# Another order of the pieces of a fused attention and gated-convolution kernel, with one more pair's exponentials done row by row on ScalarE

## The chip, the cores and the metric

The kernel runs on one core of a Trainium2 chip. The metric is the device time of one execution in microseconds (us), the median of several runs. A profiled execution has a span (from the first to the last instruction of the core) and a time of its own, which is about 2 us longer.

## The reference, cut to what matters

```python
# 8 batches, 8 heads, 576 tokens, 64 values a head; chunks of 64 tokens
scores = scale * np.matmul(q_c, k_c.transpose(0, 1, 2, 4, 3))      # 64 x 64 a chunk and head
scores = scores - np.max(scores, axis=-1, keepdims=True)
attn = np.exp(scores)
attn = attn / (np.sum(attn, axis=-1, keepdims=True) + 1e-09)
out = np.matmul(attn, v_c)                                         # all heads side by side: x
for k in range(5):                                                 # causal convolution along the tokens
    gate_pre += conv_w[k] * xp[:, k:k + S, :]
gate = 1.0 / (1.0 + np.exp(-gate_pre))
result = (gate * (x @ w_val)) @ w_out                              # 512 x 512 weights, fp32
```

## The kernel before

The 4608 tokens are cut into nine groups of 512 (g, 0 to 8) and the 512 columns into two halves of 256 (p, 0 and 1). A group and a half make a **pair**. The work is written as some thousand **pieces**, and a table, `ORDER`, lists them in the order in which they are recorded; on each engine the instructions stand in that order, and semaphores do the rest. A second table, `SLOTS`, gives each new tile its place in SBUF (z), in PSUM (b, four double banks) and among the two buffers of exponentials (e). What a piece does, by its letters:

- `lq`, `lk`, `lv`, `lw`, `lc` load q, k, v, a quarter of a weight matrix (v for w_val, o for w_out), the convolution's weights. All loads and stores are issued on SyncE, in the table's order.
- `w1` to `w9`, `wa`, `wb`, `wc`, `Q` split a weight into a high part (`v_hi`, `o_hi`) and a low part (`v_lo`, `o_lo`).
- `S g p b` makes the scores of half a pair on TensorE (16 small matmuls of 64 by 64, which the hardware runs as 32). `mx` takes the maxima on VectorE. Then one of two ways: `sb`, `ex`, `sm` subtract on VectorE, take one wide exponential on ScalarE, and sum and invert on VectorE; or `ng`, `ea`, `rc` negate the maxima on VectorE, take the exponential on ScalarE in 16 instructions, one for each block of 64 columns, each of which also leaves its sum, and add 1e-9 and invert on VectorE. `nm` multiplies by the inverse (GpSimd, or VectorE as `nmD`).
- `T` transposes on TensorE, `ec` copies out on ScalarE, `A` multiplies by v on TensorE (64 small hardware matmuls for a pair).
- `xr` (ScalarE) and `xd` (VectorE) split x into high and low, `xc` keeps it for the convolution. `k0`, `k`, `kx`, `kk` are the five taps of the convolution, `hc` and `hb` hand the last tokens of a group on, `sg` is the sigmoid.
- `V g m c` multiplies by w_val: three matmuls of 512 columns (high by high, low by high, high by low), or one of them where a fifth number stands. `vc` copies the result out, `gs` multiplies by the gate, `gr` and `gd` split that into high and low, `P g t c` multiplies by w_out (three matmuls), `oc`, `o1` copy out, `st`, `s1` store.
- `W n m` is n matmuls of 512 columns and m of 64 on zeros. They stand at the start, before there is data.

A D at the end of a name puts a piece on VectorE that is else on ScalarE or GpSimd. In the trace almost all instructions have the line of the helper that records them (L139); they are told apart by their tiles: `b<-z,v_hi` is V, `b<-o_hi,z` is P, the matmuls `b<-z,z`, `b<-z,ys`, `b<-ys,z`, `b<-ys` of 64 by 64 are S and A, `b<-ident,z` is T, `e_row<-b,mx` is `ea`, `rs<-e_row` is `sm`.

## Time and profile before

| | |
|---|---|
| median of three runs | 280.42 us (280.19 to 280.89) |
| the profiled execution, its own time | 280.77 us |
| its span | 278.7 us |
| granted TensorE clock, mean | 0.999 |
| busy: TensorE matmul / VectorE / ScalarE / GpSimd | 97% / 86% / 71% / 21% |
| chain that ended last | TensorE 90% of the span |

An engine's busy time is what its instructions cover; matmuls overlap in the records, so TensorE at 97% says only that it was hardly ever without one in flight. The rows on which the prediction rests stand further on, word for word.

### The profile page before, as it was taken

The page shows a single profiled execution, that of the slowest core. Times are in us where ns is not written, and L with a number is a line of the kernel's source. Part 1 is how long each engine was busy: PE and PEld are TensorE (multiplying, and loading weights), DVE is VectorE, ACT ScalarE, POOL GpSimd, SP SyncE. Part 2 cuts the span into 40 slices and gives each one's busy share as a digit, 9 for nine tenths or more (in the row PEclk, how much of TensorE's full clock was granted, in tenths as well). Part 3 has the DMA queues.
Part 4 walks back from the last instruction along what each step waited for, and adds up shares of the span by engine and source line. Part 5 has one row for each costly group of instructions (what it writes and reads, how often), then busy time and mean ns, then how long its engine had stood idle before and what let it go on. Part 6 is the DMA issues. An engine that isn't in the chain of part 4 may idle for free.

```text
span 278.7 us, 7853 instructions
## 1 busy us (share of the span) xinstructions
PE 269.3 (97%) x3370; PEld 216.7 (78%) x3370; DVE 240.6 (86%) x305; ACT 198.2 (71%) x366; POOL 59.5 (21%) x58
## 2 busy tenths in 40 slices
PE   8589999999999999999999999999999999999995
PEld 3357788887887878798888888888888888888884
DVE  3999999999999989988998998999999998996020
ACT  5989999999988998895968588828634544614402
POOL 1056242059293003062325001100000000300000
PEclk9999999999999999999999999999999999999999
DMA  6999999763821449440081000000000000050656
GB/s 226 394 407 406 407 409 405 301 231 121 308 104 67 162 157 368 158 154 6 2 308 70 2 5 2 0 0 2 0 0 0 4 0 0 23 205 0 245 206 226
DMA packets 14754, 42.46 MB, mean 152 GB/s; under 512 B 1536, under 2 KB 1792, under 8 KB 14720
## 3 DMA queue, kind: packets, MB, share of 16 engines
q1 hardware_dynamic: 14720, 41.97, 40.3%
q8 instruction: 26, 0.43, 0.6%
q14 instruction: 8, 0.07, 0.1%
HBM read 32.53 MB, written 9.44 MB: 151 GB/s over the span
## 4 chain that ended last, share of the span: by engine, by line
PE 90%; DVE 4%; DMA 2%; ACT 1%; issue 1%; SPq 0%; DVEq 0%; ACTq 0%
PE b L139 90%; DMA z<-in_moe_w_val 2%; ACT e_row L139 1%; DVE z L139 1%; DVE rs L139 1%; DVE mx L139 1%; DVE e_row L139 1%; SPq L139 0%; ACT z L139 0%; DVE cw_h L139 0%; DVE cw_t L139 0%; DVEq L139 0%; DVE v_hi L139 0%; ACTq L139 0%
## 5 line engine op out<-in xcount | busy, mean ns | idle before, releaser
L139 PE MATMUL b<-z,v_hi 128*128 128x512 f32 x288 | 97.3, 403 | 0.8 <-issue 0.6
L139 PE MATMUL b<-o_hi,z 128*128 128x512 f32 (+1 forms) x296 | 94.5, 390 | 0.0
L139 DVE SCALAR_TENSOR_TENSOR ys<-ys,cw 128x511 f32<-128x511 f32 (+7 forms) x104 | 84.5, 863 | 0.1
L139 ACT COPY z<-b 128x1024 f32<-128x1024 f32 (+2 forms) x53 | 50.2, 969 | 37.6 <-PE b L139 34.9
L139 PEld LDWEIGHTS b<-o_hi,z 128*128 128x128 f32 x296 | 55.1, 188 | 12.7
L139 PEld LDWEIGHTS b<-z,v_hi 128*128 128x128 f32 x288 | 53.8, 188 | 14.0 <-issue 1.4
L139 PE MATMUL b<-o_lo,z 128*128 128x512 f32 (+1 forms) x148 | 57.4, 388 | 0.0
L139 PE MATMUL b<-z,v_lo 128*128 128x512 f32 x144 | 55.9, 394 | 0.0
L139 POOL TENSOR_TENSOR z<-e_row,rs 128x1024 f32<-128x1024 f32 (+1 forms) x15 | 27.0, 1804 | 46.4 <-DVE rs L139 20.0
L139 PEld LDWEIGHTS b<-o_lo,z 128*128 128x128 f32 x148 | 27.8, 188 | 5.9
L139 PEld LDWEIGHTS b<-z,v_lo 128*128 128x128 f32 x144 | 27.1, 188 | 5.4
L139 POOL TENSOR_TENSOR z<-ys,z 128x1024 fp32r<-128x1024 f32 x4 | 10.1, 2525 | 96.9 <-ACT z L139 96.9
L139 ACT ACTIVATE ys<-ys 128x1024 f32<-128x1024 f32 x16 | 16.8, 1060 | 11.0 <-DVE ys L139 10.8
L139 ACT ACTIVATE e_row<-b,mx 128x64 f32<-128x64 f32 x80 | 23.7, 354 | 0.4 <-DVE mx L139 0.4
L139 DVE TENSOR_TENSOR z<-b,z 128x1024 fp32r<-128x1024 f32 (+1 forms) x19 | 22.0, 1160 | 2.0 <-ACT z L139 1.4
L139 ACT CAST z<-ys 128x1024 fp32r<-128x1024 f32 x16 | 16.5, 1048 | 9.0 <-DVE ys L139 9.0
L139 DVE TENSOR_REDUCE mx<-b 128x16 f32<-128x1024 f32 (+1 forms) x19 | 21.5, 1139 | 1.2 <-PE b L139 1.0
L139 PEld LDWEIGHTS b<-z,z 64*64 64x64 f32 x960 | 15.6, 134 | 6.2 <-issue 2.2
L139 ACT CAST z<-b 128x1024 fp32r<-128x1024 f32 (+1 forms) x19 | 18.7, 991 | 2.1 <-PE b L139 2.1
L139 ACT ACTIVATION_READ_ACCUMULATOR e_row<-b,mx 128x1 f32 x80 | 19.7, 247 | 0.0
L139 PE MATMUL b<-z,z 64*64 64x64 f32 x960 | 17.4, 221 | 2.3 <-DMA z<-in_q 2.2
L139 ACT ACTIVATE ys<-ys,cw 128x512 f32<-128x512 f32 (+1 forms) x25 | 19.2, 812 | 0.0
(73 smaller groups left out, 309.9 us busy)
## 6 DMA issues: line engine op xcount, KB each, us to landing
out<-z SPq DMA_DIRECT2D x16, 512.0 KB, 3.7
z<-in_q SPq DMA_DIRECT2D x10, 512.0 KB, 7.1
z<-in_v SPq DMA_DIRECT2D x9, 512.0 KB, 4.8
ys<-in_v SPq DMA_DIRECT2D x9, 512.0 KB, 10.1
ys<-in_k SPq DMA_DIRECT2D x9, 512.0 KB, 6.3
z<-in_k SPq DMA_DIRECT2D x7, 512.0 KB, 9.9
ys<-in_q SPq DMA_DIRECT2D x6, 512.0 KB, 10.2
z<-in_moe_w_val SPq DMA_DIRECT2D x4, 512.0 KB, 5.4
```

The costliest lines, as they stand in the source:

```text
L139: return tc.keep_in_program_order(fn(*args, **kwargs))
```

## The change

Both tables are replaced. The pieces are the same but for these: pair 8 1 takes its exponentials row by row (`ng`, `ea`, `rc`, with `nm` on GpSimd) where it took `sb`, `ex`, `sm` and `nmD`; some pieces change their engine (`k0` of pairs 4 0, 4 1, 5 0, 5 1 go to VectorE, `kx 6 1` and `k0 8 2` leave it; `xc 6 1`, `oc 7 1`, `gd 3 1`, `waD o 1`, `wbD o 3` go to VectorE, `xc 3 0`, `oc 4 1`, `oc 6 0`, `o1 8 3`, `gd 8 0`, `wa o 3` leave it); and the zeros' matmuls are `W 12 22` where they were `W 9 22` and, later, `W 3`. The code around the tables is the same.

```diff
-ORDER = """zw,lw v 1,zr 1,zr 0,lc,zi,zs 0,zs 1,lw v 3,lw v 2,w1 v 1,w5 c 0,w1 c 0,w2 v 1,w3 v 1,w5 v 1,w4 v 1,w2 c 0,w3 c 0,w5 v 3,
-w7 v 1,w1 v 3,w6 v 1,w8D v 1,w2 v 3,w4 c 0,w3 v 3,W 9 22,Q v 1,lk 0 1 0,lq 0 1 0,w1 v 2,w4 v 3,w2 v 2,w3 v 2,w5 v 2,w6D v 3,
-S 0 1 0,lk 0 0 0,lk 0 1 1,lq 0 1 1,lq 0 0 0,lk 0 0 1,lq 0 0 1,w4 v 2,wc v 1,mx 0 1 0,w6 v 2,w7 c 0,ng 0 1 0,w7 v 2,ea 0 1 0,
...
+ORDER = """zw,lw v 1,zr 1,zi,zs 0,zs 1,lc,lw v 3,lw v 2,zr 0,lq 0 1 0,lk 0 1 0,lq 0 1 1,lk 0 1 1,w1 v 1,lk 0 0 0,w1 c 0,w3 c 0,w2 v 1,
+w3 v 1,w5 v 1,w4 v 1,w2 c 0,w7 v 1,w1 v 3,w8D v 1,w2 v 3,w3 v 3,w6 v 1,w4 c 0,w1 v 2,w2 v 2,w3 v 2,w4 v 3,w5 v 3,W 12 22,
+S 0 1 0,w7 c 0,w4 v 2,w5 c 0,w5 v 2,mx 0 1 0,w6 v 2,S 0 1 1,lq 0 0 0,lk 0 0 1,lq 0 0 1,lw v 0,ng 0 1 0,w7 v 2,ea 0 1 0,
...
-    e="0 1 0 0 0 0 1 1 0 0 0 1 0 1 1 0 1 0",
+    e="0 1 0 0 0 0 1 1 0 0 0 1 0 1 1 1 0 0",
```

Three places show what moves. The first is TensorE from the first full scores of group 1 on, some 19 to 27 us into the trace of before. Before, it reads (the rows are `S 1 0 0` and `S 1 0 1`, `A 0 1 0`, `T 0 1 1`, `V 0 2 2 0`, `V 0 3 2 1`, `A 0 1 1`, `T 0 0`, three V, `S 1 1 0`, `A 0 0`, `S 1 1 1`):

```order
L139 MATMUL b_315<-z_269,z_271 64x64 x32
L139 MATMUL b_356<-z_353,z_273 64x64 x16
L139 MATMUL b_307<-ident,z_295 128x128 x4
L139 MATMUL b_393<-z_390,v_hi 128x512
L139 MATMUL b_393<-z_390,v_lo 128x512
L139 MATMUL b_399<-z_353,z_273 64x64 x16
L139 MATMUL b_419<-ident,z_388 128x128 x8
L139 MATMUL b_393<-z_390,v_hi 128x512 x2
L139 MATMUL b_393<-z_390,v_lo 128x512
L139 MATMUL b_439<-z_373,z_375 64x64 x16
L139 MATMUL b_459<-z_434,z_377 64x64 x32
L139 MATMUL b_439<-z_373,z_375 64x64 x16
```

And now (the rows are `S 1 0 0` and `S 1 0 1`, `T 0 1 1`, `A 0 1 0`, `A 0 1 1`, `T 0 0`, seven V, `A 0 0`, `S 1 1 0` and `S 1 1 1`):

```order
L138 MATMUL b_311<-z_228,z_226 64x64 x32
L138 MATMUL b_305<-ident,z_292 128x128 x4
L138 MATMUL b_357<-z_350,z_288 64x64 x16
L138 MATMUL b_382<-z_350,z_288 64x64 x16
L138 MATMUL b_402<-ident,z_377 128x128 x8
L138 MATMUL b_414<-z_380,v_hi 128x512
L138 MATMUL b_416<-z_380,v_hi 128x512
L138 MATMUL b_414<-z_380,v_lo 128x512
L138 MATMUL b_416<-z_380,v_hi 128x512
L138 MATMUL b_414<-z_380,v_lo 128x512
L138 MATMUL b_414<-z_380,v_hi 128x512 x2
L138 MATMUL b_443<-z_436,z_427 64x64 x32
```

Seven V now stand ahead of `A 0 0`, where two then three stood on either side of `A 0 1 1` and `T 0 0`, and the two halves of `S 1 1` have moved behind `A 0 0`. Between `S 1 1 1` and `T 1 0`, the next transposes, 14 single V stood before and 13 stand now.

The second place is TensorE at 80 to 85 us, where the scores of pair 5 1 and `A 3 1` stand side by side. Before, `V 3 0 0` followed them:

```order
L139 MATMUL b_1328<-o_hi,z_1211 128x512
L139 MATMUL b_1372<-ys 64x64 x32
L139 MATMUL b_1407<-z_1367,ys 64x64 x32
L139 MATMUL b_1446<-z_1349,v_hi 128x512
L139 MATMUL b_1446<-z_1349,v_lo 128x512
L139 MATMUL b_1446<-z_1370,v_hi 128x512
```

Now `P 0 3 3` does:

```order
L138 MATMUL b_1321<-o_hi,z_1229 128x512
L138 MATMUL b_1366<-ys 64x64 x32
L138 MATMUL b_1403<-z_1362,z_719 64x64 x32
L138 MATMUL b_1321<-o_hi,z_1113 128x512
L138 MATMUL b_1321<-o_lo,z_1113 128x512
L138 MATMUL b_1321<-o_hi,z_1243 128x512
```

The small matmuls have kept their place and number; three other wide ones follow.

The third place is ScalarE at 150 to 160 us, around the exponentials of pair 8 1, with copies out of PSUM on both sides. Before (`ex 8 1` is the second row):

```order
L139 ACTIVATE ys<-ys,cw 128x512
L139 ACTIVATE e_row_65<-e_row_65 128x16x64
L139 COPY z_2351<-b_2338 128x1024
L139 COPY z_2384<-b_2224 128x1024
L139 COPY z_2389<-b_2176 128x1024
```

Now (`ea 8 1` is the third row):

```order
L138 ACTIVATE ys<-ys,cw 128x512
L138 COPY z_2334<-b_2321 128x1024
L138 ACTIVATE e_row_65,rs_2340<-b_2204,mx_2295 128x64 x16
L138 CAST z_2448<-b_2381 128x2x2x256
L138 COPY z_2467<-b_2310 128x1024
```

Sixteen instructions stand where one stood, between the copy `ec 8 0` and the copies `xr 7 0` and `vc 4 1`.

## Rows read from the trace of the kernel before

**Rows 1.** The page's busy times, its slices of 7 us each, and its list of DMA queues (packets, MB, share of 16 engines).

```profile
PE 269.3 (97%) x3370; PEld 216.7 (78%) x3370; DVE 240.6 (86%) x305; ACT 198.2 (71%) x366; POOL 59.5 (21%) x58
...
DMA  6999999763821449440081000000000000050656
...
q8 instruction: 26, 0.43, 0.6%
```

**Rows 2.** The windows of 10 us: stretch, its length, then each engine's busy time with the number of its instructions, the granted clock, the share of the DMA engines and GB/s.

```profile
0.00:10.00 10.00, 7.09 (x67) 3.27 (x67) 5.56 (x16) 6.43 (x13) 0.79 (x8) 1.00 0.80 274
10.00:20.00 10.00, 7.57 (x183) 4.91 (x176) 9.39 (x20) 8.55 (x39) 3.35 (x3) 1.00 1.04 406
20.00:30.00 10.00, 9.65 (x223) 7.72 (x224) 9.33 (x16) 9.79 (x16) 6.39 (x4) 1.00 1.03 407
...
80.00:90.00 10.00, 9.38 (x166) 7.58 (x165) 9.27 (x13) 8.15 (x11) 5.96 (x5) 1.00 0.08 27
...
150.00:160.00 10.00, 10.00 (x172) 8.44 (x170) 9.93 (x12) 6.36 (x8) 0.83 (x1) 1.00 0.01 2
```

**Rows 3.** TensorE from 80 to 86 us in the timeline (start, duration, engine, line, operation, tiles, shapes, count, and the idle time before it).

```profile
81.37 1.16 PE L139 MATMUL b<-ys 64*64 64x64 f32 x64
...
83.39 0.50 PE L139 MATMUL b<-z,v_hi 128*128 128x512 f32 x1
...
83.72 0.39 PE L139 MATMUL b<-z,v_lo 128*128 128x512 f32 x1
...
84.74 0.50 PE L139 MATMUL b<-z,v_hi 128*128 128x512 f32 x1 [0.62 <-issue]
```

**Rows 4.** DMA queue 8 in short stretches: of 28.8 to 28.9 us, of 82.0 to 82.1 us, and of 28.8 to 30 us.

```profile
q8 instruction: 1, 0.02, 64.5%
...
q8 instruction: 1, 0.02, 79.9%
...
q8 instruction: 1, 0.02, 5.4%
```

**Rows 5.** Matmuls in four of the stretches asked for (length, busy time and count of the matmuls, clock, DMA share, GB/s).

```profile
19.33:25.05 5.72, 5.26 (x143) 1.00 1.03 407
25.05:31.23 6.18, 6.12 (x142) 1.00 1.03 407
...
81.38:84.74 3.36, 2.73 (x132) 1.00 0.02 5
84.74:104.86 20.12, 20.12 (x124) 1.00 0.42 141
```

**Rows 6.** The first 31 us in the timeline.

```profile
1.19 4.67 PE L139 MATMUL b<-warm 128*128 128x512 bf16 x31 [1.19 <-DVE warm L139]
...
9.41 0.69 PE L139 MATMUL b<-z,z 64*64 64x64 f32 x32 [0.73 <-DMA z<-in_q]
...
11.36 0.31 ACT L139 ACTIVATE e_row<-b,mx 128x64 f32<-128x64 f32 x1 [0.25 <-DVE mx L139]
...
11.40 1.37 PE L139 MATMUL b<-z,z 64*64 64x64 f32 x64 [0.54 <-DMA z<-in_q]
...
11.66 0.30 ACT L139 ACTIVATE e_row<-b,mx 128x64 f32<-128x64 f32 x1
...
13.84 1.27 POOL L139 TENSOR_TENSOR z<-z,z 128x512 fp32r<-128x512 f32 x1 [12.45 <-ACT e_row L139]
13.87 1.27 DVE L139 TENSOR_SCALAR rs<-rs 128x8 f32<-128x8 f32 x1 [0.17 <-ACT e_row L139]
...
15.29 1.18 DVE L139 TENSOR_REDUCE mx<-b 128x16 f32<-128x1024 f32 x1
...
18.31 0.16 DVE L139 TENSOR_SCALAR rs<-rs 128x8 f32<-128x8 f32 x1
...
18.92 1.24 DVE L139 TENSOR_REDUCE rs<-e_row 128x16 f32<-128x1040 f32 x1 [0.21 <-ACT e_row L139]
...
20.68 1.90 POOL L139 TENSOR_TENSOR z<-e_row,rs 128x1024 f32<-128x1024 f32 x1 [0.77 <-DVE rs L139]
...
24.14 1.02 ACT L139 COPY z<-b 128x1024 f32<-128x1024 f32 x1 [0.21 <-issue]
```

**Rows 7.** The same stretch, TensorE alone, as the timeline merges it.

```profile
18.73 1.96 PE L139 MATMUL b<-z,z 64*64 64x64 f32 x96 [0.23 <-DMA z<-in_q]
...
23.00 1.06 PE L139 MATMUL b<-ident,z 128*128 128x128 f32 x8 [0.25 <-DVE e_row L139]
23.82 0.71 PE L139 MATMUL b<-z,v_hi 128*128 128x512 f32 x2
...
24.69 2.15 PE L139 MATMUL b<-z,z 64*64 64x64 f32 x128
26.77 0.50 PE L139 MATMUL b<-z,v_hi 128*128 128x512 f32 x1
...
30.14 1.03 PE L139 MATMUL b<-ident,z 128*128 128x128 f32 x8
31.23 0.74 PE L139 MATMUL b<-z,v_hi 128*128 128x512 f32 x2
```

**Rows 8.** Groups of instructions (line, engine, operation, tiles, shapes, count, busy us, mean ns of one, idle time before them): `ex`, and `k0` with `kx` on ScalarE.

```profile
L139 ACT ACTIVATE e_row<-e_row 128x1024 f32<-128x1024 f32 x13 | 13.9, 1071 | 2.9 <-DVE e_row L139 2.9
...
L139 ACT ACTIVATE ys<-ys,cw 128x512 f32<-128x512 f32 (+1 forms) x25 | 19.2, 812 | 0.0
```

## The prediction, made before the changed kernel ran

> **What bounds the kernel now.** First the page's busy times and the windows: TensorE's matmuls cover 97% of the span, and from 30 us on all of every window but that of 80 to 90 us [rows 1, 2]. The table changes no matmul: 3370 stand before and after. So the time can move only where TensorE stands still: before 31 us, at 84 us, and after its last matmul, where copy and store keep their order. The other engines count where they make it wait.

> The other place is the start. The stretch from 25.05 to 31.23 is also one block [rows 5]; its packet starts between 28.8 and 28.9 and lasts 1.03 us [rows 4], and the next matmul after the transposes that begin at 30.14 starts at 31.23, 1.35 after the packet's end [rows 7]. Eight transposes take 0.82 when nothing holds them (23.00 to 23.82 [rows 7]), so TensorE lost some 0.3 there. With the DMA engines full (share 1.03) a block takes 3.8 + 1.03 + 1.35 = **6.18 us**; the block before it took 5.72 [rows 5].

> [...]

> **The change, the start.** I follow the new order with the durations of before.
> - `S 0 1 0` waits for its q at 9.41 [rows 6]; the same bytes stand ahead of it now, so 9.4 again.
> - `S 0 1 1` started at 11.40, after its q [rows 6]. Its two transfers of 256 KB now go ahead of a third one, 0.65 us at 406 GB/s [rows 2]: 10.7.
> - One cast less stands before the first maxima on VectorE, so `ea 0 1 0` starts at about 11.0, where it was 11.36 [rows 6].
> - The maxima of pair 0 0 started at 15.29 because a tiny instruction took 1.27 us at 13.87, beside GpSimd's 1.27 at 13.84; the same instruction later takes 0.16 [rows 6]. Now it falls ahead of GpSimd's: the maxima start when `S 0 0 1` is there, 14.2, and the sums that started at 18.92 [rows 6] start at 18.0.
> - `S 1 0 0` waited for its q until 18.73 [rows 7], the fifteenth transfer; its k is now the fifteenth, so 18.7 again.
> - `nm 0 0` on GpSimd started at 20.68 [rows 6]; now at 19.5, and `T 0 0` at 21.75 (it was 23.00 [rows 7]).
> - ScalarE copies that out (24.14 for 1.02 [rows 6]) from 23.7, behind three other copies, and `A 0 0` starts at 24.8.

> So VectorE gains 0.9 us and `A 0 0` some 0.4. But TensorE counts in blocks: the block that ended 0.36 into `S 1 1 0` (24.69 + 0.36 = 25.05 [rows 7]) now ends 0.3 into `A 0 0`, at **25.1**, because two more V stand ahead of it. The next holds the rest of `A 0 0`, `S 1 1` and 13 single V, and ends at the sixth transpose of `T 1 0`: 108 of the 128 small matmuls that took 2.08 (24.69 to 26.77), 13 of the 14 V that took 3.37 (26.77 to 30.14), and 0.6 of transposes [rows 7]: 1.76 + 3.13 + 0.6 = 5.5 us. The fetch takes 6.18 if it waits in the full queues as before, 5.72 if as in the block before. I take 6.18, the nearest row, since the queues are as full in both: 25.1 + 6.18 = 31.28 against 31.23, **+0.05**. The gain goes into a longer wait for the fetch, 0.7 for 0.3. With no such wait it is 30.6, -0.65; with one 0.3 longer, +0.35.

> **The change, at 84 us.** The block starts in `S 5 1 0` as before and ends in the third matmul of `P 0 3 3` instead of that of `V 3 0 0`. The same two scores and `A` lie in between, so the work is 2.6 us again and the wait 0.8: **0**. Bounds: -0.8 if the fetch is early, +0.2 for a later packet.

> **The rest.** 16 instructions of `ea 8 1` at 0.30 from start to start (11.36 to 11.66 [rows 6]) put 4.8 us on ScalarE and take a 1.07 away [rows 8]; `sb`, `sm` and `nmD` take three of some 1.2, as the one at 18.92 [rows 6], from VectorE, and `nm` puts one of 1.9, as the one at 20.68 [rows 6], on GpSimd. Four `k0` leave ScalarE, 0.8 each [rows 8]; on VectorE they cost from nothing to as much. The other changes of engine nearly cancel. So ScalarE gets some 2 to 4 us more and VectorE up to 4 less. What covers it: ScalarE is busy 6.36 of the 10 us at 150 to 160 while TensorE stands nowhere [rows 2]. Behind `ea 8 1` wait `xr 7 0` and `vc 4 1`, for which `T 7 1` needs the bank; by the order V pieces of 0.7 fill the time and about 1 us is left. If that cover is gone, each us late is a us: bounds 0 and +1. Value **0**. The wide matmuls go from small ones and back about as often (22 runs of small ones in each table): **-0.1**.

> **The sum.** Against the profiled execution: 280.77 + 0.05 + 0 + 0 - 0.1 = 280.7. Its time is 0.35 over the median of the runs, 280.42. So the median should be **280.4**.

> **The rivals.**
> 1. *The fetches no longer hold TensorE*: packets that start early let the block of `T 1 0` end at its work, 30.6, and that of `P 0 3 3` at 2.6. -0.65 - 0.8 - 0.1: **278.9**. For it: a block took 5.72 once, and packets start 0.65 after a block's end in quiet queues. Against it: the loads keep the queues full (share 1.03 to 50 us [rows 1, 2]), and at 84 us nothing was left to be quieter (share 0.02 [rows 5]).
> 2. *The clock falls in the new gap; slower.* `W 12 22` ends at about 6.4: nine matmuls of 0.43 to 5.0, three of half that, 22 short ones. From there to 9.41 TensorE has nothing; before, it had `Q v 1` in that stretch and `W 3` behind the first scores, and the granted clock stayed up [rows 2]. [...] It decides if the clock is down at 18.7. For it: 3 us without work is more than any stretch of before. Against it: the rows show no fall at all, though TensorE did little from 5.86 (1.19 + 4.67) to 9.41 [rows 6]. [...]
> 3. *Another block is squeezed; slower.* From `S 7 0 0` to `P 2 3 3` the new order has 26 + 32 + 64 small matmuls and six wide ones: 122 x 0.0163 (2.08/128) + 6 x 0.24 = 3.4 us, just over the 3.36 that a fetch needs. If stores or loads still fill the queues at 128 us, the fetch needs up to 6.2, and TensorE stands 2.8: **283.2**. For it: the queues were 4 to 9 tenths full from 105 to 125 us [rows 1], and transfers may now come later. Against it: they were all but empty from 125 to 139.

> **How the numbers follow.** Not told from no change by a measurement of this kernel: 0.3%, 0.84 us. Forecast, 280.4 with 279.6 to 281.2: 0.45. Rival 1: 0.27. Rival 2: 0.12. Rival 3: 0.08. Left: 0.03 faster, 0.05 slower by some copy that comes late. Faster 0.30, same 0.45, slower 0.25. The range goes 0.4 beyond the middle of rivals 1 and 2, 278.5 to 282.8: a quarter of rival 1 lies below it, a third of rival 2 and all of rival 3 above, two in ten in all.

> **What would show it.** Right: `S 0 1 1` at 10.7, `T 0 0` at 21.7, `A 0 0` at 24.8, and the matmul behind `T 1 0` at 31.3 after an "issue" wait of over 0.5; a gap of 0.8 inside `P 0 3 3`; no other gap. Wrong: a clock row under 1.00 before 25 us, a matmul behind `T 1 0` before 30.9, no gap at 84, or TensorE idle at 130 or at 155 to 165 us.

## The result, and the profile after

The changed kernel takes 284.26 us, the median of nine runs (282.44 to 285.68), beside 281.15 us (280.19 to 282.23) for nine runs of the kernel before. The ratio is 1.0100 with a 95% interval of 1.0075 to 1.0125: slower, by 2.8 us by the ratio and 3.1 by the medians, and above the range that was given. The profiled execution of the changed kernel took 283.07 us, its span is 281.3 us, 2.6 more than before.

The page of the changed kernel, busy times and the slices of the granted clock:

```profile
PE 269.6 (96%) x3370; PEld 217.4 (77%) x3370; DVE 235.5 (84%) x305; ACT 202.4 (72%) x397; POOL 65.4 (23%) x58
...
PEclk9799999999999999999999999999999999999999
```

TensorE's busy time is what it was [rows 1], 0.3 us apart; VectorE has 5.1 us less, ScalarE 4.2 and GpSimd 5.9 more. What is longer is what TensorE waits. The table of its waits (waited for, us in total, times, longest), first of the changed kernel:

```profile
PE b L138 <- DMA z<-in_k: 3.9, 2, 3.2
PE b L138 <- ACT z L138: 1.5, 2, 0.8
PE b L138 <- DVE warm L138: 1.2, 1, 1.2
PE b L138 <- issue: 1.1, 1, 1.1
PE b L138 <- POOL z L138: 0.7, 1, 0.7
```

and of the kernel before:

```profile
PE b L139 <- DMA z<-in_q: 2.2, 4, 0.7
PE b L139 <- DVE warm L139: 1.2, 1, 1.2
PE b L139 <- DVE e_row L139: 1.1, 2, 0.9
PE b L139 <- ACT v_hi L139: 0.8, 1, 0.8
PE b L139 <- issue: 0.6, 1, 0.6
PE b L139 <- DVE cw_h L139: 0.2, 1, 0.2
```

8.4 against 6.1 us: with the 0.3 of busy time this is the whole 2.6. Three places are new.

**The start.** The window of the changed kernel that follows the records of the clock (length, busy times with counts, granted clock, DMA share, GB/s):

```profile
10.91:14.32 3.41, 3.41 (x34) 1.61 (x24) 2.78 (x10) 2.47 (x16) 0.51 (x1) 0.50 1.05 406
```

For 3.41 us the granted clock is 0.50; before, it was 1.00 there [rows 2]. TensorE ahead of it and in it (`S 0 1 0`, three of the four matmuls of `Q v 1`), and `T 0 0`:

```profile
9.21 0.70 PE L138 MATMUL b<-z,z 64*64 64x64 f32 x32 [3.21 <-DMA z<-in_k]
...
11.40 2.07 PE L138 MATMUL b<-z,ident 128*128 128x512 f32 x2
12.49 1.42 PE L138 MATMUL b<-v_hi,signed 128*128 128x512 f32 x1
...
23.24 1.09 PE L138 MATMUL b<-ident,z 128*128 128x128 f32 x8 [0.72 <-POOL z L138]
```

TensorE was idle for 3.21 us ahead of `S 0 1 0`. `Q v 1` then fills 11.40 to 14.26, twice what it takes with the clock up (1.5 us, below), and `S 0 0 0` waits behind it; `T 0 0` comes at 23.24, where 21.75 was expected.

**A wait for the program near 40 us.** `S 2 0 0` and the first six matmuls of `S 2 0 1`, then the rest; and, from 38.0 to 38.1 us, DMA queue 8, which carries the program's packets:

```profile
38.64 0.81 PE L138 MATMUL b<-z,z 64*64 64x64 f32 x38
40.58 0.62 PE L138 MATMUL b<-z,z 64*64 64x64 f32 x26 [1.14 <-issue]
```

```profile
q8 instruction: 1, 0.02, 63.9%
```

The idle time is 1.14; against the usual distance of starts (that of the same two kinds of matmul elsewhere in the trace) the loss is 1.34. The block that ends here began at 31.70 (counted off, 256 instructions to a block), so it lasted 8.88 us; its packet started 6.3 us after its beginning, landed at 39.07, and TensorE went on 1.5 us later. At 84 us, where before 0.79 was lost [rows 3], nothing is lost now (`A 3 1`, then `P 0 3 3`, whose three matmuls start 0.34 and 0.23 apart):

```profile
84.30 1.11 PE L138 MATMUL b<-z,z 64*64 64x64 f32 x64
85.34 0.50 PE L138 MATMUL b<-o_hi,z 128*128 128x512 f32 x1
85.68 0.39 PE L138 MATMUL b<-o_lo,z 128*128 128x512 f32 x1
85.91 0.63 PE L138 MATMUL b<-o_hi,z 128*128 128x512 f32 x2
```

**A late store.** SyncE's row at 119 to 121 us (`lk 7 1`, and `st 0 0` as the first of two stores), then ScalarE (`xc 4 1`, `xr 4 1`), then TensorE (`T 6 1`, `V 4 0 0`):

```profile
118.71 0.33 SPq L138 DMA_DIRECT2D z<-in_k  x1
...
119.60 1.73 SPq L138 DMA_DIRECT2D out<-z  x2
```

```profile
124.52 1.02 ACT L138 COPY ys<-b 128x1024 f32<-128x1024 f32 x1
127.76 1.01 ACT L138 CAST z<-b 128x1024 fp32r<-128x1024 f32 x1 [2.22 <-DMA out<-z]
```

```profile
137.09 1.06 PE L138 MATMUL b<-ident,z 128*128 128x128 f32 x8
138.99 0.50 PE L138 MATMUL b<-z,v_hi 128*128 128x512 f32 x1 [0.83 <-ACT z L138]
```

`st 0 0` stands behind `lk 7 1` in SyncE's row. That load waits 9 us for its place, so the store, whose tile ScalarE finished at 108.16, is issued at 119.60. `xr 4 1` writes into that tile's place and waits 2.22 us for it; the exponentials and sums of pairs 6 0 and 6 1 follow it on ScalarE and VectorE, and TensorE loses 0.26 ahead of `T 6 1` and 1.08 ahead of `V 4 0 0`, measured by the usual distance of starts.

The profiled execution adds up: at the block's start behind `T 1 0` +0.47 (31.70 for 31.23), near 40 us +1.34, at 84 us -0.79, at 137 us +1.34, together +2.4 of 2.6.

### The profile page after: what moved, and what is told of

Its sections match the earlier page's. It is cut to its first block, busy times and chain, and to the rows that moved or that the text cites. A ratio compares the mean times of both kernels' runs of the same rounds, so it can differ in the third digit from the quotient of the medians.

```text
span 281.3 us, 7887 instructions
## 1 busy us (share of the span) xinstructions
PE 269.6 (96%) x3370; PEld 217.4 (77%) x3370; DVE 235.5 (84%) x305; ACT 202.4 (72%) x397; POOL 65.4 (23%) x58
## 4 chain that ended last, share of the span: by engine, by line
PE 92%; DMA 2%; ACT 1%; issue 1%; SPq 1%; DVE 1%; POOL 1%; ACTq 0%
PE b L138 92%; DMA z<-in_k 2%; SPq L138 1%; ACT z L138 1%; POOL z L138 1%; DVE mx L138 0%; DVE z L138 0%; ACT v_lo L138 0%; DVE rs L138 0%; ACTq L138 0%; DVE e_row L138 0%
## 5 line engine op out<-in xcount | busy, mean ns | idle before, releaser
L138 PE MATMUL b<-z,v_hi 128*128 128x512 f32 x288 | 96.3, 402 | 0.8 <-ACT z L138 0.8
L138 PE MATMUL b<-o_hi,z 128*128 128x512 f32 (+1 forms) x296 | 93.3, 390 | 0.0
L138 DVE SCALAR_TENSOR_TENSOR ys<-ys,cw 128x510 f32<-128x510 f32 (+7 forms) x104 | 86.5, 877 | 0.2
L138 POOL TENSOR_TENSOR z<-e_row,rs 128x1024 f32<-128x1024 f32 (+1 forms) x17 | 31.1, 1833 | 53.4 <-DVE rs L138 28.4
L138 ACT ACTIVATE e_row<-b,mx 128x64 f32<-128x64 f32 x96 | 28.5, 351 | 0.7 <-DVE mx L138 0.7
L138 ACT CAST z<-ys 128x1024 fp32r<-128x1024 f32 x17 | 17.5, 1047 | 12.0 <-DVE ys L138 12.0
L138 DVE TENSOR_REDUCE mx<-b 128x16 f32<-128x1024 f32 (+1 forms) x19 | 21.7, 1149 | 5.0 <-PE b L138 4.7
L138 PE MATMUL b<-z,z 64*64 64x64 f32 x1024 | 18.6, 221 | 5.2 <-DMA z<-in_k 3.9
L138 ACT ACTIVATION_READ_ACCUMULATOR e_row<-b,mx 128x1 f32 x96 | 23.4, 245 | 0.0
L138 PEld LDWEIGHTS b<-z,z 64*64 64x64 f32 x1024 | 16.7, 136 | 8.3 <-issue 7.0
L138 ACT CAST z<-b 128x1024 fp32r<-128x1024 f32 (+1 forms) x19 | 18.7, 992 | 5.0 <-PE b L138 2.6
L138 PE MATMUL b<-ident,z 128*128 128x128 f32 x144 | 19.1, 274 | 1.4 <-POOL z L138 0.7
## 6 DMA issues: line engine op xcount, KB each, us to landing
ys<-in_v SPq DMA_DIRECT2D x7, 512.0 KB, 10.2
```

Of the source, the lines that this page charges most:

```text
L138: return tc.keep_in_program_order(fn(*args, **kwargs))
```

## The experiments

Where two experiments are compared, it is by their distance to the kernel before on the same chip. Every change is to the two tables alone.

### The changed kernel again

> The changed kernel once more, as it is, for a second trace. Theory: its losses against the kernel before belong to the order, so this trace has them again: a granted clock of 0.5 somewhere between 10 and 15 us, Q v 1 taking some 2.9 us, a wait with "issue" as its releaser inside S 2 0 1 near 40 us (1.3 us), and the waits of T 6 1 and V 4 0 0 at 137 to 139 us (1.26 us together). 284.3. Rival: the wait near 40 us is an accident of one execution (the packet came 6.3 us after the block's start there, where 3.0 to 3.8 is usual): then it is missing here, and the time of this trace is some 1.3 us shorter unless the slow stretch is longer.

Measured: 283.87 us (282.69 to 284.79), ratio 1.0083 (1.0054 to 1.0111). The loads land 1.2 us later in this trace; the granted clock is 0.50 from 8.8 to 15.6 us, and the wait near 40 us is there again, 1.34. So it is no accident. The waits at 137 us are gone, although `xr 4 1` still waits 0.96 us for the store; but one for the program has come four us later, inside `S 7 1 1`, also of 1.34:

```profile
142.95 0.58 PE L138 MATMUL b<-z,ys 64*64 64x64 f32 x24 [1.14 <-issue]
```

Its packet started 4.7 us after its block, though the DMA queues were all but empty from 132 to 139 us (share 0.01). What held it is not shown.

### The gap filled

```diff
-W 12 22
+W 26 8
```

> The changed kernel with W 26 8 for W 12 22: as many matmuls on zeros, 34, so every block of the program begins where it did, but they last until about 8.9 us and fill the gap ahead of S 0 1 0 at 9.2. Theory (the clock falls because of the gap): granted clock 1.0 throughout, Q v 1 in 1.3 us instead of 2.9, S 0 0 0 at about 12.7 instead of 14.26, and 1.1 to 2 us less: 282.3 to 283.2. Rival (it is the new order at the start, Q v 1 behind the scores, that is late, and the clock only shows in stretches where TensorE waits anyway): 284.3, within 0.4.

Measured: 283.11 us (281.21 to 284.76), ratio 1.0061 (1.0031 to 1.0090); 0.76 less than the changed kernel beside it. `S 0 1 0`, `Q v 1`, `T 0 0`, and then the matmuls behind the waits at 32 and 40 us:

```profile
10.23 0.69 PE L138 MATMUL b<-z,z 64*64 64x64 f32 x32 [0.25 <-DMA z<-in_k]
...
12.20 1.12 PE L138 MATMUL b<-z,ident 128*128 128x512 f32 x2
...
22.93 1.09 PE L138 MATMUL b<-ident,z 128*128 128x128 f32 x8 [0.72 <-POOL z L138]
...
32.13 0.38 PE L138 MATMUL b<-ident,z 128*128 128x128 f32 x2 [0.44 <-issue]
...
40.36 0.62 PE L138 MATMUL b<-z,z 64*64 64x64 f32 x26 [0.49 <-issue]
```

In this trace the clock stays at 1.00, `Q v 1` takes 1.5 us, and from `S 0 1 0` to `T 0 0` are 12.70 us, where the changed kernel has 14.03: 1.3 gained. (Against the start of the trace little of it is seen, since the loads land 1.0 us later here; the span is 281.4.) At the block behind `T 1 0`, 0.6 of it goes into a wait for the packet, as the prediction had said of its own gain there; but the wait near 40 us is shorter for it, 0.7, and TensorE goes on there 30.13 us after `S 0 1 0`, where it was 31.37. The rival, that the clock does not matter, does not fit this trace. The size, 1.2 in the trace, is at the lower end of what was expected, and in the runs below it; there the zeros did not always help, for four of the ten runs have a mean granted clock of 0.994, the others 1.000.

### The store ahead of the load that waits

```diff
-lv 7 1,lk 6 1,lq 8 0,lk 7 1,lv 7 0,st 0 0
+lv 7 1,st 0 0,lk 6 1,lq 8 0,lk 7 1,lv 7 0
```

> The changed kernel with the store st 0 0 moved ahead of the load lk 6 1 in SyncE's row. In the trace of the changed kernel oc 0 0 is done at 108.16, but its store is issued at 119.60, behind lk 7 1, which waits 9.1 us for TensorE; xr 4 1 (ScalarE) writes into the place of oc 0 0's tile and waits 2.2 us for that store, and ex 6 0, ex 6 1, sm 6 1, nm 6 1, T 6 1 follow it. Theory: with the store issued at about 109, xr 4 1 starts at 125.6 instead of 127.76 and the waits of T 6 1 and V 4 0 0 at 137 to 139 us (0.26 + 1.0) go: 283.0. Rival: the next in line is as late (xd 4 1 waits for st 1 1, or sb 6 1 on VectorE is what ex 6 1 waits for), and the time stays at 284.3, within 0.4.

Measured: 282.98 us (282.28 to 283.50), ratio 1.0061 (1.0042 to 1.0080); 0.89 less than the changed kernel beside it. `xr 4 1` no longer waits (it starts behind `xc 4 1`), and `T 6 1` and `V 4 0 0` follow without a gap:

```profile
126.08 1.04 ACT L138 CAST z<-b 128x1024 fp32r<-128x1024 f32 x1
```

```profile
137.48 1.03 PE L138 MATMUL b<-ident,z 128*128 128x128 f32 x8
138.27 0.48 PE L138 MATMUL b<-z,v_hi 128*128 128x512 f32 x1
```

In none of the eight traces of this order with the store moved is there a wait between 100 and 145 us; of the three without it, each has one of 1.3 us, at 137 or at 141. Only the one at 137 is a wait for the store. In the two traces with the other, `xr 4 1` waits 1.0 us for the store and TensorE loses nothing by it; what the store has to do with the late packet is not shown.

### The gap put into the kernel before, and the same gap filled

Only the start on TensorE is taken from the change, `wc v 1` moving with its `Q`:

```diff
-W 9 22,Q v 1 ... S 0 1 0 ... W 3,S 0 1 1,w8D v 2,S 0 0 0
+W 12 22 ... S 0 1 0 ... S 0 1 1,Q v 1,w8D v 2,S 0 0 0
```

> The kernel before with only the new start on TensorE: W 12 22 for W 9 22 and W 3 (34 matmuls either way), and Q v 1 behind S 0 1 1 instead of ahead of S 0 1 0. All else is the order of before. Theory (clock): TensorE has nothing from about 6 to 9.4 us, the granted clock shows 0.5 for 3 us or more before 15 us, and S 1 1 1 is 0.7 to 2.5 us late: 281.9 to 283.7 against 281.2. Rival (order): the clock stays 1.0, and only what Q v 1 lies on the path counts, 0 to 0.5: 281.2 to 281.7.

The second kernel has `W 26 8` for `W 12 22`:

> The kernel of the run before (the kernel before with the new start on TensorE), but with W 26 8 for W 12 22, so that zeros fill most of the gap; as many instructions. Theory (clock): granted clock 1.0 from 10 us on, Q v 1 in about 1.3 us instead of 2.7, and 281.2 to 281.8. Rival (the later Q v 1 itself is what costs): it stays at 282.8, within 0.4.

Measured: with the gap 282.76 us (281.44 to 283.73), ratio 1.0051 (1.0027 to 1.0075), 1.68 above the kernel before; filled 281.53 (280.37 to 283.11), ratio 1.0034 (1.0005 to 1.0063), 0.41 above. The first two matmul groups of `Q v 1` and `T 0 0`, with the gap:

```profile
13.37 2.07 PE L138 MATMUL b<-z,ident 128*128 128x512 f32 x2
...
25.09 1.07 PE L138 MATMUL b<-ident,z 128*128 128x128 f32 x8 [0.31 <-DVE e_row L138]
```

and filled:

```profile
12.24 1.12 PE L138 MATMUL b<-z,ident 128*128 128x512 f32 x2
...
23.12 1.06 PE L138 MATMUL b<-ident,z 128*128 128x128 f32 x8 [0.32 <-DVE e_row L138]
```

From `S 0 1 0` (10.32 and 9.62) to `T 0 0` are 14.77 and 13.50 us. So in the old order the slower clock costs 1.27 us in the trace, and the medians of the runs lie as far apart. The runs say more. With the gap, all ten have a mean granted clock of 0.987 or 0.988. Filled, five of ten have 1.000 and take 280.4 to 281.0 us; the other five have 0.992 to 0.994 and take 282.1 to 283.1. So the zeros hold the clock up in half of the runs only, and where they do, the later `Q v 1` costs nothing that can be told from the kernel before. The 1.8 us between the halves need not be the clock's alone: with loads that land later the gap is longer too (in the two traces of the changed kernel 3.82 against 3.21 us, with the loads 1.2 us later).

### Both edits

> The changed kernel with both edits that were tried alone: W 26 8, and st 0 0 ahead of lk 6 1. Theory (two losses in two places, so they add): 0.8 and 0.9 off 284.0, 282.2, with the wait of 1.3 near 40 us left. Rival (the wait moves: with the start earlier the packet that came in time at 134 comes late, and 1.3 is lost at 140 us as in the run with the filled gap): 283.1.

Measured: 281.69 us (281.03 to 283.31), ratio 1.0027 (1.0002 to 1.0052), and once more on another chip:

> The kernel with the two edits once more (W 26 8, and st 0 0 ahead of lk 6 1), for a comparison with the two above on one chip: 0.2 to 0.6 above the kernel before, with the wait of 1.3 near 40 us and none at 84 us or at 137 us.

281.64 us (280.96 to 284.05), ratio 1.0035 (1.0007 to 1.0062). 0.5 above the kernel before, where the changed kernel is 2.8 to 3.1 above: the two edits give back 2.2 to 2.6, somewhat more than the sum of their single gains (0.76 and 0.89). Neither single gain is clear of the intervals by itself; both together are (1.0062 at most here, 1.0075 at least for the nine runs of the changed kernel).

### The blocks shifted

```diff
-W 26 8
+W 26 12
```

> As the one before, but W 26 12: four more short matmuls on zeros, 0.12 us, so that every later block of TensorE's program begins 8 instructions, some 0.9 us of wide matmuls, earlier in the work. In the four traces of this order the packet that is late (5.8 to 6.5 us after the block's start at 32 us, where 3.7 is usual) belongs to a block that begins within 0.4 us of a packet of another engine on queue 14; in the traces of before's order those are 0.9 to 1.2 apart, and the packet comes after 3.7 to 4.0. Theory (the other engine's packet holds it up): now the block begins 0.9 us earlier, the packet comes by 3.7 to 4 us after it, the wait of 1.3 near 40 us goes, and the time is 1.3 below the kernel without the shift: 280.9 to 281.3. Rival (it is the loads of that stretch that hold it up, until 38 us): the packet starts at 38 again, the wait near 40 us grows to 2.2, and the time is 283.

Measured: 281.67 us (280.76 to 282.39), ratio 1.0019 (0.9998 to 1.0039): no better than without the shift. The block at 32 us did not begin earlier against the other engine's packet, because it waited for its own (0.44); the late packet came 6.4 us after it again. So this run doesn't tell the two theories apart, and both times that were expected of it were wrong.

### The loads paused

SyncE's row, where `lq 5 1` waits for `A 1 1` (46 us), with the loads that are put behind it:

```diff
+A 1 1,lq 5 1,lv 2 1,lk 3 1,lq 3 1,lk 4 0,lq 4 0,lq 4 1,lv 3 0,lv 3 1,lv 8 0
```

> The changed kernel with the gap filled (W 26 8) and st 0 0 ahead of lk 6 1, and besides with lq 5 1, whose place is free only after A 1 1 (46 us), moved up in SyncE's row, and nine loads that are needed from 60 us on (lv 2 1, lk 3 1, lq 3 1, lk 4 0, lq 4 0, lq 4 1, lv 3 0, lv 3 1, lv 8 0) behind it: SyncE then issues nothing from about 30 to 46 us, and the DMA queues are empty from about 34 us. The block that begins at 32 to 33 us is the one whose successor's packet started 5.8 to 6.5 us after it in all six traces of this order. Theory (the loads in the queues hold the packet up): it starts within 3.5 us, the wait of 1.3 near 40 us goes, and so does any at 47 us: 280.4 (1.3 off the 281.7 of the kernel with the two edits). Rival (something else holds that packet up, such as what TensorE or another engine does at that time): it starts 6 us after the block's start again, and the time is 281.7.

> As the run with the pause in SyncE's loads, but lq 4 1, lv 3 0, lv 3 1 and lv 8 0 go further back, behind lk 4 1 (57 us). In that run the wait near 40 us was gone, but one of 0.56 stood at 61 us instead: its packet came 3.2 us after the block's start at 56 us, behind the loads that had been put off to 46 to 57 us. Theory (loads in the queues hold a packet up, wherever they are put): with four loads fewer before 57 us that packet comes within 1.5 us, no wait at 40 or 61 us, and 1.3 less than the kernel with the two edits alone, on the same chip. Rival (the time taken out there comes back in a wait of another kind): as the kernel with the two edits, within 0.4.

```diff
-lq 5 1,lv 2 1,...
+lq 5 1,lk 3 0,lq 3 0,lv 2 0,lv 2 1,...
```

> As the run with the pause and four loads further back, but lk 3 0, lq 3 0 and lv 2 0 too stand behind the pause, so that SyncE issues its last load before it at about 26 us instead of 30.5. In the run before, all loads that moved until 39 us had been issued before 30.5 us, and the late packet started at 39.0, when they were through. Theory (the packet stands in line behind the loads that were issued before its block begins at 32.7, some 8 us deep): now they are through by 35.2 us, the packet starts by then, 2.5 us after its block's start or less, no wait near 40 us; 1.3 less than the kernel with the two edits, 280.3 to 280.6 against 281.1 to 281.2 of the kernel before. Rival (that packet is late for another reason): it starts 6 us after its block again, the wait of 1.3 stays, 281.6.

Measured, in this order: 282.14 us (281.52 to 283.46), ratio 1.0041 (1.0024 to 1.0058); 281.65 (280.76 to 283.09), ratio 1.0015 (0.9993 to 1.0038), beside 281.64 for the two edits alone on that chip; 281.25 (280.21 to 283.00), ratio 1.0003 (0.9982 to 1.0024). The first, 1.3 above the kernel before, is slower than the two edits alone were on other chips (0.5), though its trace has lost the wait near 40 us; why is not shown. In the first two, SyncE's last load before the pause goes out at 30 us, but the queues are about 8 us deep and empty only at 38 to 39; the packet started at 38.06 and 39.02, 5.1 and 6.3 us after its block, and the wait of 1.3 was gone in one trace and there in the other. In the third the queues empty at 35 to 37 us (windows, DMA share next to last), the packet starts at 37.23, 3.8 us after its block, and `S 2 0 1` runs through:

```profile
30.00:34.00 4.00, 4.00 (x23) 3.37 (x22) 4.00 (x7) 3.83 (x7) 1.80 (x1) 1.00 1.03 407
34.00:38.00 4.00, 4.00 (x19) 3.07 (x17) 4.00 (x8) 4.00 (x24) 0.00 (x0) 1.00 0.27 104
```

```profile
40.35 1.16 PE L138 MATMUL b<-z,z 64*64 64x64 f32 x64
41.44 0.74 PE L138 MATMUL b<-z,v_lo 128*128 128x512 f32 x2
...
62.51 0.85 PE L138 MATMUL b<-ys 64*64 64x64 f32 x42 [0.55 <-issue]
```

The next two packets come 0.5 us after and 0.4 us ahead of their blocks' starts, where the two traces of the two edits alone have 3.8 and 4.0, then 2.5 and 3.7. So the loads do hold the packets up. But the loads that were put off fill the queues later, and there the packets are late: 0.75 is lost at 62 us and 0.28 at 69 us. Of 1.3 us some 0.3 is left in the trace. The runs, level with the kernel before where the two edits alone are 0.5 above, fit that, but the intervals overlap.

### Pair 8 1 alone, either way

In the kernel before, row by row:

```diff
-sb 8 1 ... ex 8 1 ... sm 8 1 ... nmD 8 1
+ng 8 1 ... ea 8 1 ... rc 8 1 ... nm 8 1
```

> The kernel before with one part of the change alone: pair 8 1 takes ng, ea, rc and nm where it took sb, ex, sm and nmD. Theory (the copies behind it on ScalarE have the time): ScalarE gets some 4.8 us for 1.07 at 151 us, TensorE waits nowhere between 150 and 165 us, 281.1 within 0.3. Rival: vc 4 1 and vc 4 0, or T 8 1 behind a multiplication that now takes 1.9 on GpSimd, come late: TensorE waits up to 1 us there, 282.

and the reverse of it in the changed kernel with both edits:

> The changed kernel with the gap filled and st 0 0 ahead of lk 6 1, and with pair 8 1 back at sb, ex, sm and nmD, in the places of ng, ea, rc and nm: the one part of the change that is no new order, undone in the new order. Theory (in this order T 7 1 stands far enough behind for the sixteen instructions to be hidden): no wait of TensorE at 150 to 170 us either way, 281.7 within 0.3. Rival (ScalarE's 4 us or GpSimd's 1.9 are paid somewhere after 160 us): 280.7 to 281.2.

Measured: in the old order 287.38 us (four runs, 286.10 to 287.88), ratio 1.0228 (1.0183 to 1.0272), 6.3 slower. In the new order, undone, 282.61 (281.73 to 285.14), ratio 1.0068 (1.0043 to 1.0093), 1.76 above the kernel before where 0.5 was: 1.2 slower. All four times expected were wrong. The old order: `sb 8 1` in the kernel before, then with the rows the last instruction of `ea 8 1`, `T 7 1`, and the window around it:

```profile
149.69 1.23 DVE L139 TENSOR_TENSOR e_row<-b,mx 128x1024 f32<-128x1024 f32 x1
```

```profile
155.42 0.42 ACT L138 ACTIVATE e_row<-b,mx 128x64 f32<-128x64 f32 x1
```

```profile
151.15 0.40 PE L138 MATMUL b<-z,v_hi 128*128 128x512 f32 x1
156.04 1.94 PE L138 MATMUL b<-ident,z 128*128 128x128 f32 x8 [4.49 <-issue]
```

```profile
154.00:158.00 4.00, 1.96 (x9) 1.99 (x10) 1.99 (x4) 1.94 (x14) 0.00 (x0) 0.50 0.00 0
```

By the old table `T 7 1` writes into the bank of pair 8 1's scores. `sb` had read them by 150.91; `ea` reads the last of them until 155.85. TensorE stands for 4.7 us. The clock falls inside that wait, at 153.7, and is back 6.8 us later, so the first 4.5 us of the work behind run at half of it. By the new table `T 7 1` has another bank; the piece that takes the one of pair 8 1's scores is `A 6 1`, which starts at 160.61, 0.7 us after the last of `ea 8 1` (159.87), and waits for nothing. There the wide way is the late one: VectorE has `nmD 8 1` at 163.45 ahead of `xd 7 0`, for which ScalarE's copy `vc 4 1` waits 0.83 until 165.90, and TensorE's `T 8 1` and `A 8 1` wait for copies in turn:

```profile
166.97 1.09 PE L138 MATMUL b<-ident,z 128*128 128x128 f32 x8 [0.21 <-ACT ys L138]
...
170.68 1.16 PE L138 MATMUL b<-z,ys 64*64 64x64 f32 x64 [0.59 <-ACT z L138]
```

These two cost 0.37 and 0.79 us against the usual distance of starts, together the 1.2. (The 0.5 is from other chips, so the trace is the better witness here.)

### The kernel before with its blocks shifted

```diff
-W 9 22
+W 10 13
```

> The kernel before with W 10 13 for W 9 22: eight matmuls on zeros fewer, so that every later block of TensorE's program begins 16 instructions further on in the work; nothing else is changed. Theory (the waits at 31 us and at 84 us come from where a block of 256 instructions begins against the short work): the block at 81 to 85 us now has 120 small matmuls and eight wide ones more, 4.3 us of work for the 3.4 that its packet needs, so the wait of 0.78 goes, and the 0.23 at 31 us too: 0.8 to 1.0 less, 280.1 to 280.3 against 281.1. Rival (the fetch holds TensorE for a time of its own): a wait of the same size elsewhere, 281.1 within 0.3.

Measured: 280.44 us (279.84 to 281.01), ratio 0.9972 (0.9956 to 0.9989), 0.72 less, a little under the 0.8 to 1.0 expected. `A 3 1` and `V 3 0 0`, where 0.79 was lost [rows 3], start 0.34 and 0.23 apart:

```profile
82.82 1.11 PE L138 MATMUL b<-z,ys 64*64 64x64 f32 x64
83.86 0.50 PE L138 MATMUL b<-z,v_hi 128*128 128x512 f32 x1
84.20 0.39 PE L138 MATMUL b<-z,v_lo 128*128 128x512 f32 x1
84.43 0.39 PE L138 MATMUL b<-z,v_hi 128*128 128x512 f32 x1
```

The wait behind `T 1 0` is gone too. This is the fastest version of all: the old order, with eight matmuls on zeros fewer.

## Why the prediction was wrong, point by point

- **The forecast (no change, 280.4): wrong**, slower by 2.8 us or more. The second rival, the clock, is what happened at the start, but it is only one of three losses; the other two stand in no rival. Of the 3.8 us between forecast and measurement another 0.7 is the base: 280.42 was the median of three runs, nine give 281.15.
- **The clock, valued as a rival.** It was said to decide if the clock is down at 18.7 us, until when TensorE still waits for loads [rows 6, 7]. That step failed: in the first trace the clock was back at 14.32, and it cost 1.3 us of `T 0 0` all the same, since the doubled `Q v 1` (2.86 us for 1.5) stands ahead of `S 0 0 0` and `S 0 0 1`, and everything from the maxima of 0 0 on follows those. The middle of this rival, 282.4, on which the range's upper end of 282.8 rests, was the author's estimate: no row and no run shows its 2.0 us above the forecast; the traces show 1.3 in the new order and 1.27 in the old. Its chance of 0.12 rested on a stretch of before in which TensorE had `Q v 1` to do, and that is just what the change took away. Nor did the clock stay up in every run of the kernel before: of its 121 runs beside these experiments 53 have a mean granted clock of 0.994 or less, and their median is 281.3, where that of the others is 280.8.
- **The sum at the start: right, under a clock that stays up.** From `S 0 1 0` to `T 0 0` it had 21.75 - 9.41 = 12.34; with the gap filled it is 12.70. To the block behind `T 1 0` it had 31.28 - 9.41 = 21.87; filled, it is 32.13 - 10.23 = 21.90, and the gain goes into a wait for the program there, 0.6, as it said.
- **The next block: the term that was left out.** The working stopped at 31.28 and took every later block in full queues to be no longer than 6.18, a bound from two rows. That step failed: the next one needed 8.88 for 7.5 of work, +1.34. The third rival had this mechanism, in another place. That the loads hold the packet up is shown by the pause; why by 6.3 us is not. From 28 to 38 us a load lands 10.2 us after its issue in both kernels (the median), and before, the packet of the block at 31.23 came only 3.7 us after the block's start.
- **84 us: the place right, the size wrong.** It had 0.8 before and after, since the same 2.6 us of work lie between. Now the packet starts at 83.17, 0.16 ahead of the block, where before it was 0.65 behind [rows 4]. That a packet starts only after its block's beginning was the step that failed; the trace of before has cases against it, such as the packet at 111.34 for the block that begins at 114.15 (counted off). That the place of the block makes the wait is shown by the shifted kernel before.
- **The rest, valued at 0 with +1 at most: +1.34 in the first trace.** It was looked for at ScalarE's sixteen instructions, which in this order turned out to be a gain of 1.2. The loss came from SyncE's row: "copy and store keep their order" was taken of the end alone, and the store of `oc 0 0` was not followed past the loads that it is queued behind. In the other two traces with that store in its place the loss is as large, but it is a late packet's.
- **The third rival** did not happen: no wait at 130 us.

## What to carry to other kernels

Follow a store in its queue past every load in front of it, and ask what waits for its place: a load that waits for room holds up all that stand behind it (here `lk 7 1`, for 9 us, and `st 0 0` with it, whose tile was finished at 108.16 and which was issued at 119.60). Where an engine fetches its program in blocks, as TensorE does here in 26 packets of 16 KB [rows 1], their alignment is a term of its own: count the instructions between the stretches of small work, and shift them by a few dummy instructions before moving any real work. (Here one shift of sixteen instructions gained 0.7 us, and one of eight in the other order gained nothing.) And an edit's price belongs to the order it stands in: the same edit was worth 1.2 us in one order and cost 6.3 in the other.

## What the runs showed of the hardware that was not expected

- After the gap of 3 to 4 us the granted clock was 0.50 for 3.4 us in one execution of the changed kernel and for 6.8 in another (the clock's records), and for 6.8 in the two other kernels with that gap; the changed kernel's times scatter over 3.2 us, those of the kernel before over 2.0. Inside a wait of 4.5 us at 151 us the clock fell as well, to 0.50 for 6.8 us. Behind the longer zeros, it stayed up in four of nine traces, in one over a wait of 1.4 us, and fell for 3.4 us in five, over waits of 1.0 to 1.3. Of all runs with the longer zeros 70 of 98 have a mean granted clock of 0.998 or more, of the 35 with the gap none.
- The windows show a granted clock of 1.00 from 0 to 10 us, yet the first zeros start 0.43 us apart and later ones 0.21, in the changed kernel from 4.1 us on, with the gap filled from 7.0 on. So the windows do not show that slower stretch.
- Behind 20 us, the 16 traces have 28 waits of 0.2 us or more that begin a block, and counted off, all stand, within three, at the same place modulo 256 of TensorE's instructions, semaphore instructions included. Packets started up to 4.9 us ahead of the first matmul of the block before their own (in stretches of wide matmuls), and with full queues up to 6.5 us behind it. Where TensorE waited for one, it went on 1.3 to 1.6 us after the packet's end.
- At 140 us, in two of the traces, a packet came 4.7 us after its block with the DMA queues all but empty (share 0.01 from 132 to 136 us in the second trace of the changed kernel, 0.00 from 136 to 140). What held it stays open.
